# A written-out order of some 1,860 tasks for attention and a gated feed-forward layer on one core: the same tasks in another order, some evictions on another engine, buffers in other slots

## The chip, the cores and the metric

The kernel runs on one core of one Trainium2 chip. The core has engines that each run their own list of instructions in order: TensorE (PE in the profile) multiplies matrices, VectorE (DVE) and ScalarE (ACT) work on the results, GpSimd (POOL) does small elementwise work and issues transfers, SyncE (SP) only issues transfers. Engines meet at semaphores alone: an instruction that waits holds everything behind it on its engine. The metric is the device time of one launch in microseconds (us). Lower is better.

## The reference

Causal attention over 4 batches of 768 tokens with 8 heads of 64 columns, and then a gated layer on the 3072 tokens:

```
mask   = heads 0, 2, 6: all keys up to the query
         other heads:   keys 0 to 3 (sinks), and the last 64 keys
a      = softmax(q k^T / 8, masked)
x      = a v                                    (3072 tokens x 512)
out    = x + sigmoid(x w_res) * ((gelu(x w_gate) * (x w_val)) w_out)
```

with w_gate and w_val of 512 x 1536, w_out of 1536 x 512 and w_res of 512 x 512, all in float32. The kernel computes in float16 with float32 sums.

## The kernel before, in words

**Tiles and stages.** The tokens go in six chunks of 512. A chunk has two halves: *attention* (scores, exp, masks, weighted sums of v, division by the softmax sum, which gives x in token order) and *feed-forward*. Between them x is cast to float16 and turned into feature order (xT), half of it by TensorE transposes (`xT`, L1063) and, in chunks 3, 4 and 5, the other half by a transposing transfer that SP issues (`xD`, L1054). The first chunk's attention is the start of the program; later attention is laid among the feed-forward matmuls of the chunk before it, so that TensorE always has something to do. From the second chunk on, the large products (x with w_gate and w_val, h with w_out) are partly done as seven products of half-size blocks in place of eight, with sums of blocks made on DVE (`wS`, `xS`, `hS`). The gate (`gelu`, `tanh`) is on ACT, the product with the other branch on DVE.

**What is loaded when.** All q, k, v and weight loads are issued by POOL, in its own order (L539). For the first two chunks q and k are turned by TensorE (L682); later ones by transposing transfers on SP (L726). A shifted copy of v, `vs`, is needed where the 64-key window crosses a tile: for the first tiles it is made by DVE or ACT (L617), from the second chunk on by transfers that SP issues (L633). The rows of v for the four sink keys are copied into a small buffer `vk`; for batch 0 these four copies are POOL's (L598), and they need that DVE has cleared that buffer (the memset at L532).

**What sets the order.** `Graph.add` collects tasks, each with an engine, what it depends on and the buffers that it uses. Tasks that could run on two engines (evictions from PSUM, casts, copies) carry alternatives. The string `PLAN` lists every task by number, in one global order; the letter after a number is the engine that is chosen for a task with alternatives (a ACT, d DVE, g POOL, s SP), and `wN` puts N filler matmuls (256 columns of zeros, L1414) on TensorE. `PLACES` gives every buffer its slot in its pool, in the order in which buffers first appear. `schedule` appends each task to its engine's list in the order of `PLAN`; each engine then runs its list in order, and `assign_waits` adds only the semaphore waits that the dependences and the reuse of buffers need.

**Tilings.** A matmul that may run in two halves of 64 columns (`mm`, L477 whole, L478 as a pair) takes the tiling that TensorE is in when its turn comes, so the order also decides where TensorE changes its tiling.

Of the kernel before, what the change touches and what calls it, by code (L numbers as in the profile page):

```python
# [51 lines left out]
    "1 0 14 214 16 210 211 212 215 2 5 w39 240 213 241d w2 228 216 229a w4 230 236 231d 217 237d w6 411 3 6 232 412 4 233d "  # L52
    "200 w4 408 242 409 7 w1 234 243d 238 8 235a 9 239d 10 219 w5 414 410 w1 476 415 11 222 425 416 223 419 224d 426 221 "
    "420 417 422 218 418 225d 427 428 478 421 459 423 477 220 429 424 199 430 w3 442 460 443 413 471 444 431 245 445 432 "
    "472 w1 449 446 447 433 450 255 451 464 462 448 465 434 452 201 453 463 w4 467 461 202 13 435 468 w4 455 436 479 480 "
    "481 466 203 457 456a 437 w1 438 440 458a 482 439d 204 441d w1 473 226d w1 523 474 483 454 205 539 484 538 475 254 227d "
    "522 485 244 503 470 524 505 469 504 540 252 525 207 506 486 541 496 253a 497 488 507 498 206 499 487 514 500 489 501 "
    "266 516 490 17 530 491 267a 256 494 511 531 495d 246 532 492 515 493d 208 502 509 546 508 510a 552 512d 247 533 534 "
    "517 554 209 536 527 556 257 542 558 268 547 548 280 553 550 281 549 526 551 269 555 528 570 529 535 543 537 572 15 576 "
    "594 574 578 544 588 580 545 577 598 559 557 571 590 582 573 584 575 579 586 561 560 564 562 610 592 563 566 581 264 "  # L60
    "568 250 611 265d 296 518 290 589 520 251d 565 287 567 519 289 569 262 198 690 521 295 687 691 12 679 248 591 599 259a "
    "277 680 583 593 585 276 602 688 621 597 293 587 612 622 332 689 670 261a 676 671 674 326 600 249 613 605 623 283 675 "
    "260d 606 624 603 677 625 272 682 595 626 271 681 685 667 601 686 683 284 668 607 672 678 263 614 292 615 684 669 627 "
    "274 632 628 673 616 275 609 617 629 322 692 696 618 697 636 286 633 638 637 634 693 640 639 604 694 641 635 695 698 "
    "714 715 699 642 608 643 258d 700 644d 713 645a 703 701 704 705 649 706 702a 646 707 647 716 718 596 650 648a 709 708 "
    "717 711 710a 652 719 651 722 720 723 653 712d 724 721a 655 725 656 654 740 726 741 727 730 658 731d 728 659 657 729a "
    "747 619 746 660 620 735 770 734 630 742 736 664 631 771 737 273 738 772 752 661 744 754 739 743 662 748 732 745 774 "
    "750 278 663 749 756 775d 785 270 773 776a 777 751 786a 753 787a 755 778 282 796 779 797a 788 781 758 789 799 297 798a "
    "760 800 790 782 792 780 294 757 801 784 793 791 803 783 802 795 285 804 759 794 806 807 762 761 291 808d 805 818 763 "
    "809a 810 829 819d 288 764 811 830a 820d 821 398 831a 812 822 832 813 814 279 328 823 833 824 299 825 306 834 815 298 "  # L70
    "836 835 329 816 826 837 827 848 817 300 828 838 766 320 849 839 765 768 307 767 665 931 397 769 850 343 840 932 852 "
    "844 853 304 851 841 922 856a 924 308 906 845 925 858 847 859 309 843 854 860a 855 842 301 923 864 857d 865 316 846 910 "
    "907 866 926 861 870 911 871 862 914 927 863 928 875 867 929 874 868 909 876 881 310d 908 915 917 912 869 317 882 877 "
    "913 916 342 918 872 934 935 303 936 937 920 878 919 331 942 933 921 938 879 873 939 940 885a 943 323 944 318 880 887 "
    "945 888 946 941a 325 956 952 883 889a 930 957 958 319 884 947 948 953 333 959 949a 954 955 950 960 963 951a 961 965 "
    "315 964 893 886a 966 962a 894 967 330 890 312a 891 313d 895 971 892 969 972a 899 968 666 896 970a 314 897 900 305 976 "
    "1011 981 898 975 327 977 978 979 982 302 980 984 988 311d 1013 983 1012 1015 324 1014 985 987 986 989 990 345 1016d "
    "991 1026 973 992 1018 1027a 993 1017a 995 334 1019 1029 321 904 997 1037 1020 1038a 1021 1022 1028a 994 1030 1039a "
    "1023 903 1040 1024 1031 905 1041 996 1025 1032 998 1042 1048 1033 1000 1044 335 1049a 1034 1045 1035 1043 999 1036 "
    "1046 1051 1001 1047 1050d 1059 1052 1003 1070 1060d 1002 901 1061a 1062 1071a 1054 902 1063 1072a 1005 1004 1064 360 "  # L80
    "1073 1066 1053 1065 1074 336 1007 1055 1075 337 1056 1077 1067 1076 1058 1068 371 1078 1089 1069 1079 347 1009 1057 "
    "1006 1090 358 1008 1080 733 1091 369 1010 384 1166 1081 1093 1167 383 1085 1094 1082 1092 1153 400 1151 1097d 1154 "
    "1159 1095 1086 357 1099 1084 1152 1100 1083 361 1096 1101a 1156 1088 1098a 1163 394 1157 1087 1105 1106 404 1102 1164 "
    "1107 1103 1158 1111 1112 1160 1104 1147 1116 1161 1115 1108 1148 1109 1155 1117 1118 1110 1162 1149 340 1188 1150 1177 "
    "1119 1168 1113 349 1178 1122 1165 1173 1169 1170 1171 350 1179 1172 1189 1184 1185 1120 1174 1180 368 1175 1123 1181 "
    "372 1121 1186 1190 1195 1126d 401 1191 365d 1187 1176d 1124 1125 1192 1114 1183 1182 1197 1128 1127a 1129 1193 1196 "
    "1131 1130a 1198 1132 1194a 370 1199 1134 1135 1133 1203 1136 1201 338 1137 1204d 1202a 1138 1140 1139 1141 1200 1219 "
    "373 1214 1142 1208 1243 1143 1213 359 1145 1220 1245 339 1244 1215 1216 1217 346 1207 1218 1221 354 1222 1246 1223 "
    "1209 355 1210 1224 1211 385 1231 1212 1258 395 1269 1259a 1247 348 1270a 1225 1260a 1248d 1271a 1227 1249d 1250 344 "
    "1272 1251 1261 1233 1273 367 1252 1262 1235 1253 1254 351 1263 1144 1264 1265 1255 1274 1257 1226 366 1276 1266 1206 "  # L90
    "1256 1275 399 1268 1229 1228 1267 1280 1277 341 1281d 1237 1279 1230 1239 974 1282a 1291 1278 352 1283 1238 1292a 1284 "
    "356 1302 1293d 1294 1303a 1285 1295 1240 1241 1205 1287 1305 1304a 1296 1242 1286 353 1306 1288 380 1297 1298 1308 "
    "1289 376 1307 1299 1309 1321 1146 1301 1290 1300 1310 379 1232 1322 1312 1234 388 1311 1402 1323 392 1236 1403 1317 "
    "403 1325 1313 1324 1326 377 363d 1387 1314 1329a 1385 1399 1386 1327 1318 1388 1331 364d 1316 1332 1328 1320 1400 "
    "1333d 1379 1383 1315 1337 1330a 374 1380 1338 1319 1334 381 1401 1335 1384 1339 1393 1390 1381 1343 1336 396 1391 1344 "
    "1382 1404 1340 1348 1405 362a 1389 1406 1394 378 1407 1408 1409 1341 1410 1354 1411 1355 1413 1342 405 1412a 1397 "
    "1358d 1395 1392 1415 1396 1414 1356 1416 1360 1417 1361 1398 1357 1347 1419 1420 1424 1362d 1359a 1349 1425 1418 1421 "
    "1422 1423 1426 1427 1366 1428 1363 1429 375 1367 1364 1430a 1368 1431 1365 1432 1433 1372 1434 1369 1435 1370 1373 "
    "1371 1437 1439 1438a 1350 1440d 1436 1444 1351 1481 1450 1345 1452 1374 1455 1346 1443 1479 513 1445 391 1446 1447 382 "
    "1449 1448 1461 1375 1451 1480 1457 1453 389 1483 1454 1463 1484a 1456 1459 1485d 1486 1465 1458 1487 1679 1494 1442 "  # L100
    "1460 1462 1495a 1482 1488 1464 1490 1489 1496d 1491 1466 1497 1493 1505 390 1498 1467 1492 1499 1506a 1469 1501 386 "
    "1508 1507d 1471 1500 1509 1441 1502 1516 1503 402 1510 1517a 1511 1504 1518a 1468 1512 1519 393 1527 1520 1470 1528a "
    "1513 1529a 1472 1521 1530 387 1515 1522 1523 1514 1473 1531 1524 1538 1525 1533 1539a 1526 1475 406 1532 1540d 1477 "
    "1541 1474 1534 407 1542 1476 1535 1543 1536 1352 1545 1537 1478 1544 1353 1549 1640 1546 1377 1557 1376 1548 1378 1641 "
    "1559 1547 1558 1550 1633 1560 1621 1631 1553 1634 1561 1552 1562 1563 1554 1565a 1564 1556 1632 1567 1551 1568 1566d "
# [1405 lines left out]
```

## Time and profile before

| | |
|---|---|
| time, median of 3 runs | 265.75 us (265.31 to 266.03) |
| profiled execution, span | 264.3 us |
| its time outside the span, by the median | 1.45 us |
| PE busy | 254.5 us (96%) in 3421 matmuls |
| DVE busy | 210.8 us (80%) in 473 instructions |
| ACT busy | 155.3 us (59%) in 274 |
| POOL busy | 106.8 us (40%) in 145 |
| granted TensorE clock, mean | 0.997 of full |

The page divides the span into 40 slices of 6.6 us and gives the busy share of each engine in tenths. An engine's "busy" leaves out the issue of transfers on SP. A row of the waits says which engine stood idle, before which line, and whose end let it go on. The timeline gives the start and the length of groups of instructions in us from the start of the span.

### The profile page before, as it was taken

To read this page: it belongs to the slowest core of one execution; us is meant where nothing else is said; L and a number is where in the kernel's file an instruction comes from. 1 tells how busy PE (TensorE), PEld (TensorE's weight loads), DVE (VectorE), ACT (ScalarE), POOL (GpSimd) and SP (SyncE) were. 2 spreads that over 40 slices of the span, in tenths; PEclk is the share of its full clock that TensorE was granted. 3 is DMA by queue.
4 is the path that set the end of the run, shared out by engine and by line. 5 is a ranking of instruction groups with operands and counts; after the bars stand their busy time and mean duration, and the time that the engine had idled before them with its cause. 6 is when DMAs were issued, how large, how long until landed. Compare 5 with 4: busy or idle time off the path is not lost.

```text
span 264.3 us, 8077 instructions
## 1 busy us (share of the span) xinstructions
PE 254.5 (96%) x3421; PEld 180.7 (68%) x3421; DVE 210.8 (80%) x473; ACT 155.3 (59%) x274; POOL 106.8 (40%) x145
## 2 busy tenths in 40 slices
PE   8999999999999999999998899999999998999993
PEld 5657655558567578667677477579588677778891
DVE  1499555999988978678999677999687976877985
ACT  1277534964554998564883356884655995445511
POOL 8996741990000998013976620711500111110021
PEclk9999999999999999999999999999999999999998
DMA  7999999999297999968999994899589509050004
GB/s 69 166 139 178 207 196 191 188 158 115 82 271 99 141 123 135 182 154 182 136 97 124 152 138 93 200 123 104 69 92 237 101 2 122 7 77 2 2 2 159
DMA packets 102067, 33.17 MB, mean 125 GB/s; under 512 B 88720, under 2 KB 97168, under 8 KB 102032
## 3 DMA queue, kind: packets, MB, share of 16 engines
q0 software_dynamic: 74704, 18.88, 77.3%
q1 hardware_dynamic: 26896, 13.26, 25.0%
q8 instruction: 27, 0.44, 0.7%
q10 hardware_dynamic: 432, 0.52, 0.5%
q14 instruction: 8, 0.07, 0.1%
HBM read 29.36 MB, written 10.49 MB: 151 GB/s over the span
## 4 chain that ended last, share of the span: by engine, by line
PE 87%; DVE 8%; DMA 3%; issue 1%; ACT 0%; DVEq 0%
PE ps L477 45%; PE ps L478 30%; PE ps L850 4%; PE ps L1414 4%; DMA xT<-x 3%; PE ps L682 2%; PE ps L974 2%; PE ps L1063 1%; DVE xtok L1041 1%; DVE x L1039 1%; DVE vk L598 1%; PE ps L941 1%; DVE hS L1251 0%; DVE hT L1228 0%; DVE vs L617 0%
## 5 line engine op out<-in xcount | busy, mean ns | idle before, releaser
L539 POOL DMA_DIRECT2D qks<-in_q_dram x37 | 33.2, 983 | 48.3 <-DMA qT<-qks 26.1
L1359 POOL DMA_DIRECT2D out_dram<-otile x16 | 15.6, 975 | 76.8 <-DVE otile L1355 66.2
L477 PE MATMUL ps<-xT,wg 128*128 128x512 f16 (+1 forms) x172 | 38.7, 337 | 1.4 <-DMA xT<-x 1.0
L477 PE MATMUL ps<-xT,wv 128*128 128x512 f16 (+1 forms) x172 | 38.5, 337 | 0.0
L1129 ACT ACTIVATE gact<-ps 128x512 f16<-128x512 f32 x38 | 22.1, 596 | 27.0 <-PE ps L477 18.0
L1131 DVE SCALAR_TENSOR_TENSOR hT<-gact,ps 128x512 f16<-128x512 f16 x38 | 25.8, 683 | 13.7 <-ACT gact L1129 5.8
L539 POOL DMA_DIRECT2D qks<-in_k_dram x37 | 34.8, 977 | 1.4 <-POOLq L1493 0.8
L1203 DVE TENSOR_TENSOR ps<-ps,otile 128x256 f32<-128x256 f32 x60 | 24.0, 428 | 7.7 <-PE ps L477 3.7
L1221 ACT ACTIVATE gact<-ps 128x512 f16<-128x512 f32 x30 | 16.6, 596 | 15.7 <-PE ps L477 10.8
L539 POOL DMA_DIRECT2D va<-in_v_dram x24 | 23.7, 1017 | 3.8 <-DVE va L534 3.8
L477 PEld LDWEIGHTS ps<-xT,wg 128*128 128x128 f16 x172 | 16.2, 98 | 13.1 <-DMA xT<-x 1.5
L477 PEld LDWEIGHTS ps<-xT,wv 128*128 128x128 f16 x172 | 16.6, 98 | 11.4 <-issue 0.2
L866 ACT ACTIVATE ea<-ps 128x1024 f16<-128x1024 f32 (+2 forms) x24 | 22.0, 925 | 1.4 <-PE ps L850 1.3
L1228 DVE SCALAR_TENSOR_TENSOR hT<-gact,ps 128x512 f16<-128x512 f16 x30 | 19.3, 682 | 2.6 <-PE ps L478 1.2
L1299 ACT ACTIVATE srs<-ps 128x512 f32<-128x512 f32 x22 | 13.1, 599 | 12.2 <-PE ps L478 7.8
L477 PE MATMUL ps<-wo,hT 128*128 128x256 f16 (+1 forms) x114 | 18.3, 296 | 0.0
L478 PE MATMUL ps<-xT,wg 128*64 128x512 f16 (+1 forms) x144 | 17.6, 344 | 0.0
L478 PE MATMUL ps<-xT,wv 128*64 128x512 f16 (+1 forms) x144 | 17.6, 344 | 0.0
L1041 DVE TENSOR_TENSOR xtok<-ps,rcp 128x512 f32<-128x512 f32 (+1 forms) x28 | 16.8, 608 | 0.6
L1331 DVE TENSOR_TENSOR otile<-otile,ps 128x256 f32<-128x256 f32 x33 | 13.1, 412 | 3.7 <-PE ps L477 2.4
L850 PE MATMUL ps<-qT,kT 64*128 64x64 f16 (+4 forms) x391 | 15.9, 213 | 0.1
L478 PE MATMUL ps<-wo,hT 128*64 128x256 f16 x216 | 15.6, 273 | 0.4 <-DVE otile L1325 0.4
(175 smaller groups left out, 590.4 us busy)
## 6 DMA issues: line engine op xcount, KB each, us to landing
out_dram<-xtok SPq DMA_DIRECT2D x4, 1024.0 KB, 4.8
out_dram<-otile POOLq DMA_DIRECT2D x16, 256.0 KB, 4.5
va<-in_v_dram POOLq DMA_DIRECT2D x24, 128.0 KB, 5.6
qks<-in_k_dram POOLq DMA_DIRECT2D x32, 64.0 KB, 4.9
qks<-in_q_dram POOLq DMA_DIRECT2D x32, 64.0 KB, 5.0
wv<-in_moe_w_val_dram POOLq DMA_DIRECT2D x3, 512.0 KB, 13.2
wg<-in_moe_w_gate_dram POOLq DMA_DIRECT2D x3, 512.0 KB, 11.4
wo<-in_moe_w_out_dram POOLq DMA_DIRECT2D x4, 384.0 KB, 20.9
```

What stands on the lines that cost most here:

```text
L477: return e.matmul(o, lhsT=lhsT, rhs=rhs, **k)
L478: return [e.matmul(o[h:h + 64], lhsT=lhsT[:, h:h + 64], rhs=rhs, **k) for h in (0, 64)][-1]
L539: return G.add(eng, issue, lambda e: e.dma_start(out_ap(), in_ap), deps, prio, bufs=bufs, dma=cost, name=name, grp=grp)
L850: return [e.matmul(at(scr)[:, oo:oo + w], lhsT=side(BB, qb, low, 1)[half, k0:k0 + 128], rhs=side(BB, qb, low, 0)[half, qq:qq + w], start=T ...
L866: return e.activation(out=o, in_=i_, func=AF.Exp, scale=SM_SCALE)
L1041: t2 = G.add("dve", c_dve(2 * n * 64), lambda e: e.tensor_tensor(out=xview(), in0=avv(0, DHEAD), in1=scale(), op=ALU.mult), [t1] + xdeps, ...
L1129: ta = G.add("act", c_act(512), (lambda gb=gb, ga=ga, gw=gw: lambda e: e.activation(out=at(ga)[:, :], in_=at(gb)[:, gw], func=AF.Gelu))(), ...
L1131: th = G.add("dve", c_dve(512), (lambda vb=vb, ga=ga, f=f, vw=vw: lambda e: e.scalar_tensor_tensor(out=hv(f), in0=at(ga)[:, :], scalar=0.5 ...
L1203: return G.add("dve", c_dve(256), lambda e: e.tensor_tensor(out=at(ps)[:, o], in0=at(ps)[:, BL], in1=at(es)[:, 0:256], op=ALU.add), deps, ...
L1221: ta = G.add("act", c_act(512), (lambda x=x, ga=ga, both=both: lambda e: e.activation(out=two(at(ga)[:, :]), in_=both(x), func=AF.Gelu))() ...
L1228: th = G.add("dve", c_dve(512), (lambda x=x, f=f, ga=ga, both=both: lambda e: e.scalar_tensor_tensor(out=two(hv(f)), in0=two(at(ga)[:, :]) ...
L1359: t = G.add("pool", 1.0, (lambda ot=ot, r0=r0: lambda e: e.dma_start(out[r0:r0 + 128, :], at(ot)[:, :], accum_op=ALU.add))(), ends + [stor ...
```

## The change

Two tables of numbers are replaced, `PLAN` and `PLACES`. No task is added to the work or taken from it, except fillers: 55 in place of 77. The first lines of the two tables, which stand for all of them:

```diff
 PLAN = (
-    "1 0 14 214 16 210 211 212 215 2 5 w39 240 213 241d w2 228 216 229a w4 230 236 231d 217 237d w6 411 3 6 232 412 4 233d "
+    "0 210 16 211 213 212 1 2 w20 228 230 w3 234 214 17 231 229a 411 235 408 412 5 232 233 w12 419 215 409 240 6 3 7 217 4 "
...
 PLACES = (
-    "0 2 0 0 0 1 0 0 1 1 1 2 3 0 0 2 0 3 0 1 1 1 1 3 1 0 0 0 1 0 1 1 1 0 0 0 2 0 2 1 1 0 1 1 1 0 1 0 0 2 0 2 0 1 0 0 1 1 0 "
```

In numbers: fillers 77 to 55 (39 to 20 before the first real matmul); changes of TensorE's tiling 104 to 94, all ten of them before the first w_gate product; 22 matmuls whole before and now pairs; DVE 475 to 461 instructions and ACT 279 to 290, mostly copies that move from DVE to ACT; the last additions of the residual on POOL are in four pieces of 256 columns and one of 512, where there were two and one. The table being one line shorter, every line number of the changed kernel is smaller by one (L539 becomes L538).

**First place: POOL at the start**, which issues all loads. `qks` receives q and k, `va` is v, `wg`, `wv`, `wr`, `wo` are the four weights. Before, from the first weights on:

```order
L539 DMA wv<-in_moe_w_val_dram 128x4x512
L497 AFFINE_SELECT m_win<-m_win 128x256
L497 AFFINE_SELECT m_win<-m_win 128x64
L525 MEMSET m_win 128x64
L497 AFFINE_SELECT m_win<-m_win 128x64
L539 DMA va<-in_v_dram 128x8x64
L598 COPY vk<-va 4x130 x3
L539 DMA va<-in_v_dram 128x8x64
L598 COPY vk<-va 4x130
L539 DMA wg<-in_moe_w_gate_dram 128x4x512
L539 DMA qks<-in_q_dram 128x8x128 x2
L539 DMA wg<-in_moe_w_gate_dram 128x4x512
```

and now:

```order
L538 DMA va<-in_v_dram 128x8x64 x2
L538 DMA qks<-in_q_dram 128x8x128
L538 DMA wg<-in_moe_w_gate_dram 128x4x512
L597 COPY vk<-va 4x130 x4
L538 DMA qks<-in_k_dram 128x8x128
L538 DMA wv<-in_moe_w_val_dram 128x4x512
L538 DMA wg<-in_moe_w_gate_dram 128x4x512
L538 DMA qks<-in_q_dram 128x8x128
L538 DMA wv<-in_moe_w_val_dram 128x4x512
L538 DMA wg<-in_moe_w_gate_dram 128x4x512
```

All four copies into `vk` now stand in one place, behind the first part of w_gate and ahead of every other weight; the first part of w_val has moved behind them. The memset of DVE on which they wait is the third instruction of DVE's list before, and the 23rd now; ahead of it there now are seven evictions of q and k, masks, and copies of v.

**Second place: TensorE between the attention of chunk 3 and the first product that reads its transfer-transposed half** (`vk,ek` are the last sums that this half of x waits for, `xT,wg` and `xT,wv` the first products). Before, the last such sum stands 32 rows above the product that waits for the transfer; the last rows of this stretch are:

```order
L477 MATMUL ps<-vk,ek 128x65 x3
L477 MATMUL ps<-wo,hS 128x256 x4
L477 MATMUL ps<-wo,wS 128x256 x2
L477 MATMUL ps<-wo,hT 128x256 x6
L1063 MATMUL ps<-ident,x 128x128 x8
L477 MATMUL ps<-wo,hT 128x256 x6
L477 MATMUL ps<-wt,hT 128x256 x6
L477 MATMUL ps<-xT,wg 128x512 x2
L477 MATMUL ps<-xT,wv 128x512 x4
L477 MATMUL ps<-xT,wg 128x512 x2
L477 MATMUL ps<-xT,wv 128x512 x2
L477 MATMUL ps<-xT,wg 128x512 x2
```

and now the whole stretch, from those sums to the product that waits (the second half of the last row):

```order
L476 MATMUL ps<-vk,ek 128x65 x9
L1062 MATMUL ps<-ident,x 128x128 x8
L476 MATMUL ps<-wt,hS 128x256 x4
L476 MATMUL ps<-wt,wS 128x256 x2
L476 MATMUL ps<-wt,hS 128x256
L476 MATMUL ps<-wt,wS 128x256 x2
L476 MATMUL ps<-xT,wg 128x512 x4
L476 MATMUL ps<-wo,hT 128x256 x6
L476 MATMUL ps<-wo,hS 128x256 x4
L476 MATMUL ps<-wo,wS 128x256 x2
L476 MATMUL ps<-xT,wv 128x512 x2
L476 MATMUL ps<-wt,hT 128x256 x6
L476 MATMUL ps<-xT,wv 128x512 x4
```

The sums have moved down to just above the transposes, so that fewer matmuls lie between the end of the attention and the product. In chunk 4 the stretch shrinks likewise, from 72 to 42 half-width matmuls of 256 columns and from 84 small sums to none, with 16 of 512 columns in both; in chunk 5 from 72 and 92 to 42 and none, with 16 and 24 of 512 columns.

**Third place: SP around that transfer** (`xT<-x`). Before:

```order
L1054 DMA_TRANSPOSE xT<-x 128x8x128
L726 DMA_TRANSPOSE kT<-qks 128x4x128 x2
L726 DMA_TRANSPOSE qT<-qks 128x4x128 x2
L726 DMA_TRANSPOSE kT<-qks 128x4x128
L633 DMA vs<-va 64x2x455
```

and now:

```order
L736 DMA q<-qT 64x256
L1280 DMA out_dram<-xtok 128x4x512
L1053 DMA_TRANSPOSE xT<-x 128x8x128
L632 DMA vs<-va 64x455
L725 DMA_TRANSPOSE qT<-qks 128x4x128
L632 DMA vs<-va 64x2x455
```

The transfer is still issued once per chunk; its neighbours on SP have changed. In chunk 3 the cast of x that it needs, last of what it waits for before, has moved from DVE (L1048) to ACT (L1046).

150 rows, old and new, of tables (PLACES, PLAN) are left out of this document.

## The prediction

> **What bounds the kernel now.** I read the page first (busy shares, slices, chain), then the waits of PE, then the timeline around the longest of them.
>
> ```profile
> span 264.3 us, 8077 instructions
> PE 254.5 (96%) x3421; PEld 180.7 (68%) x3421; DVE 210.8 (80%) x473; ACT 155.3 (59%) x274; POOL 106.8 (40%) x145
> PE   8999999999999999999998899999999998999993
> PE 87%; DVE 8%; DMA 3%; issue 1%; ACT 0%; DVEq 0%
> ```
>
> PE is busy in every slice but the first and the last, and it is 87% of the chain that ended last. So time is PE's work plus what PE waits. The waits of PE (engine, tile, line; who ended the wait; us in total, times, longest):
>
> ```profile
> PE ps L1414 <- DVE blank L511: 1.2, 1, 1.2
> PE ps L478 <- issue: 1.1, 1, 1.1
> PE ps L477 <- DMA xT<-x: 1.0, 1, 1.0
> PE ps L1063 <- DVE x L1039: 0.7, 1, 0.7
> PE ps L478 <- DVE otile L1325: 0.4, 1, 0.4
> PE ps L477 <- DVE xtok L1041: 0.4, 1, 0.4
> PE ps L478 <- DVE hS L1251: 0.3, 1, 0.3
> PE ps L478 <- DVE otile L1331: 0.2, 1, 0.2
> ```
>
> They are few and short, 5.3 us together, and that is all that an order can remove; what it can add has no such ceiling. Beside them the start costs time, since PE's dense work begins only with the first w_gate and w_val products. PE's timeline, and PE's work in stretches (start:end, its length, busy us and matmuls of PE):
>
> ```profile
> 1.21 7.03 PE L1414 MATMUL ps<-blank 128*128 128x256 f16 x39 [1.21 <-DVE blank L511]
> 22.26 1.03 PE L477 MATMUL ps<-xT,wv 128*128 128x256 f16 x8
> 23.67 1.03 PE L477 MATMUL ps<-xT,wg 128*128 128x256 f16 x8 [0.38 <-DVE xtok L1041]
> ...
> 1.20:6.50 5.30, 5.29 (x25) 3.78 (x26) 1.00 0.90 84
> 6.50:8.16 1.66, 1.66 (x16) 1.30 (x13) 1.00 1.70 162
> ```
>
> Thirty-nine fillers hold PE until 8.16, where the first transposes start; the first 25 take 0.21 us each (5.29/25), the later ones 0.104 (1.66/16). From this second row I price the rest: 256 columns 0.104 us, 512 twice that, 128 half; a pair of half-width matmuls counts as one.
>
> **The change part by part.** The real matmuls are the same; so the sum starts from 264.3 and asks, place by place, which waits go and which come.
>
> *The start.* Fillers go from 77 to 55, and 20 stand first instead of 39. The cover for this is DVE, not PE:
>
> ```profile
> 2.44 0.81 POOL L539 DMA_DIRECT2D qks<-in_k_dram  x1
> 8.62 0.69 DVE L693 COPY kT<-ps 128x512 f16<-128x512 f16 x1 [6.58 <-PE ps L682]
> 14.28 0.41 DVE L902 TENSOR_TENSOR ea<-ea,m_causal 128x512 f16<-128x512 f16 x1
> 23.10 0.42 DVE L1041 TENSOR_TENSOR xtok<-ps,rcp 128x256 f32<-128x256 f32 x1
> ```
>
> (The first row is POOL's first load.) DVE starts with the first eviction at 8.62, works without a gap from 14.28, and its xtok releases the first w_gate product. Now PE reaches its first transposes some 2.3 us earlier, since 20 fillers at 0.21 end at 5.4 and the loads of q and k, whose issue starts at 2.44 either way, are the next limit. But DVE's list up to the x that this product needs is only 3 instructions shorter (34 for 37, by 0.4 us each 1.2 us at most), and behind it come a transpose and an ACT eviction. If all of the earlier start arrived, the first w_gate product would start at 23.67 - 2.3 = 21.4; if none, at 23.67. I take 23.0, nearer to the late end, since DVE has no gap in which to catch up. The work ahead of it is the same on both sides: 8 w_val products less (8 x 0.104 = 0.8 us), 16 transposes and 16 short sums more (0.8 us). Term: **-0.7**, bounds -2.3 and +0.5. It contains the 0.4 on xtok. Ten changes of tiling fewer lie in this same stretch, under DVE's cover, and count nothing.
>
> *POOL's copies into vk.* These now wait for DVE's 23rd instruction, and all weights but the first part of w_gate are queued behind them. The trace has such a stop of POOL, later:
>
> ```profile
> 12.51 0.94 POOL L598 COPY vk<-va 4x130 f16<-4x130 f16 x3
> 17.27 0.77 POOL L539 DMA_DIRECT2D wg<-in_moe_w_gate_dram  x1
> 28.09 1.78 POOL L539 DMA_DIRECT2D va<-in_v_dram  x2 [3.84 <-DVE va L534]
> ...
> wv<-in_moe_w_val_dram POOLq DMA_DIRECT2D x3, 512.0 KB, 13.2
> wg<-in_moe_w_gate_dram POOLq DMA_DIRECT2D x3, 512.0 KB, 11.4
> wo<-in_moe_w_out_dram POOLq DMA_DIRECT2D x4, 384.0 KB, 20.9
> ```
>
> DVE's work ahead of that memset is seven evictions at 0.69 (4.8), masks and copies of v (some 4.6) and gaps as before (1.6): from about 6.3 it ends near 17.5. Four copies at 0.31 (0.94/3) bring POOL to 18.8, where the second part of w_gate was issued at 17.27 before; with a k load ahead of w_val and about 0.8 us for each issue, the first part of w_val goes out near 20.5 (9.43 before) and w_gate's second near 21.3, four us later. The long times to landing (11 to 21 us) are queueing, and the queue runs empty in the stop, so much of the four us comes back. Stretched over the products in their new order this leaves each weight some 1 to 3 us ahead of its first use. Bounds 0 and +1.5 (one weight late by half its lead twice); I take **+0.2**.
>
> *The second chunk's vs copies* wait for v loads that stand behind those weights. The transfers of SP at L633 take this long to landing (min/median/max of 14):
>
> ```profile
> L633 SPq DMA_DIRECT2D vs<-va x14: 485/609/650, 46.6 to 204.3; - x14
> DMA to landing us min/median/max: 2.0/4.3/7.3
> ```
>
> Their v loads land near 55 to 56 by the same shift, so the copies at 58 to 63 by this row, and the first windowed sums come on PE at about 61. Wait: bounds 0 and 2.5, median landing 0; I take **+0.9**.
>
> *The transposed half of x.* These rows (start, length of the issue; then to landing of the three) carry the largest term:
>
> ```profile
> 142.46 1.24 SPq L1054 DMA_TRANSPOSE xT<-x  x1
> 180.85 1.23 SPq L1054 DMA_TRANSPOSE xT<-x  x1
> 221.41 1.52 SPq L1054 DMA_TRANSPOSE xT<-x  x1
> DMA to landing us min/median/max: 3.7/4.9/7.4
> 179.85 0.20 DVE L1028 RECIPROCAL rcp<-ps 128x8 f32<-128x8 f32 x1
> 180.08 0.69 DVE L1039 TENSOR_TENSOR x<-ps,rcp 128x512 f16<-128x512 f32 x1
> 149.86 0.61 PE L477 MATMUL ps<-xT,wg 128*128 128x512 f16 x2 [1.05 <-DMA xT<-x]
> ```
>
> The first took 7.4 us and PE waited 1.05 for it at 149.86; the third took 3.7. Before, 7 us and more of matmuls covered each. Now, in chunk 3, from the last sum to the waiting product lie 8 of 128 columns (0.4), 27 of 256 (2.8) and 8 of 512 (1.7): 4.9 us. Of that some 1.2 us pass before the issue (DVE's reciprocal and scaling take from 179.85 to 180.77 ahead of the issue at 180.85, and 0.2 to 0.3 go from the sum's end to their start), so 3.7 are cover. At 3.7 to landing PE waits 0, at 7.4 it waits 3.7; loads of the next chunk are still in flight there as before, but fewer right ahead of it: half, **+1.85** in place of the 1.0 that goes. In chunk 4, 21 pairs of 256 and 8 of 512 are 3.85, less 1.2 is 2.7: at 3.7 it waits 1.0, at 4.9 2.2; SP has no transpose just ahead, as at 221.41, so **+1.0**. In chunk 5 the same counting gives 5.1 - 1.2 = 3.9 of cover: 0, up to +1.0.
>
> *Other waits.* The 0.7 on x (L1039) and the 0.3 and 0.2 on hS and otile (L1331) lie where the order is wholly different, and I take them as gone: **-1.2** (0 if they come again elsewhere). ACT makes more of the copies that refill PSUM for a following sum; the shortest such loops are about 0.2 us shorter in matmuls than before: **+0.3**, up to 1. The issue stall of 1.1 and the end stay: the last products and their tail are in the same order.
>
> *Sum.* 264.3 - 0.7 - 1.0 - 1.2 + 0.2 + 0.9 + 1.85 + 1.0 + 0.3 = 265.65 us of span. The profiled execution's span stands 1.45 below the median of the runs (265.75), so the time is 267.1 us.
>
> [...] The rows show that the granted clock column reads 1.00 while the first 25 fillers run at half the later rate, up to 6.5 us. [...]
>
> **The rivals.** *One: the transfers land in time (faster).* At 3.7 us the transposed half costs 0 and 1.0, the vs copies and the weights are ahead: 265.65 - 1.85 - 0.9 - 0.2 = 262.7, and with 0.3 less in ACT's loops 262.4; time 263.9. For it: the third transfer's 3.7, and fewer transposes on SP behind the one of chunk 3. Against: 7.4 under load, and chunk 3 still has load.
>
> *Two: POOL's stop decides (much slower).* If DVE's memset comes 3 us later than worked out, or the queue does not catch up, w_val and w_out come late one after the other: from a delay beyond 3 us on, each us counts once. Two us there, 2.5 on vs and 3.7 in chunk 3: 265.65 + 1.8 + 1.6 + 1.85 = 270.9, time 272.3. For it: landing times up to 20.9 behind a full queue.
>
> *Three: the array is cold longer.* A start in which real matmuls run at 0.21 instead of 0.104 per 256 columns adds about half of 5.5 us of early PE work; DVE covers most, so the first w_gate product comes at 24.5 instead of 23.0: 267.15, time 268.6. Against it: PE has 35 more fillers to bridge gaps.
>
> *Four: no change.* What goes and what comes cancel, with 0.5 in chunk 3 where I took 1.85: 264.3, time 265.7.
>
> **How the numbers follow.** Forecast 0.36, rival one 0.34, rival two 0.10, three 0.04, four 0.16. A measurement tells 0.3% (0.8 us) from no change. Faster is rival one (0.34), same is rival four (0.16), slower the rest (0.50). The range goes from 262.2, below rival one for a start at 21.9 in place of 23.0, to 271.4, where chunk 3 waits its 3.7, vs 2.5 and chunk 4 2.2 (265.65 + 1.85 + 1.6 + 1.2 = 270.3, plus 1.45, less the 0.35 by which not all come at once). The forecast's own range is 266.5 to 269.
>
> **What would show each step.** In the changed profile: the first w_gate row near 23.0 with a wait on ACT or DVE of at most 0.5; POOL idle before `vk` for 2 us or more, released by DVE vk; waits of PE on DMA xT<-x of 1 to 3 us in two places, and one on vs near 61; none on wg, wv, wr, wo above 0.5. If PE waits for x less than 0.5 us in all, rival one is right. If waits on weights exceed 2 us, rival two. The prediction as a whole is wrong if the time lies below 265, or if a wait of over 2 us stands at a place that is not named here.

## The result, and the profile after

The changed kernel takes **276.56 us** (median of 4 runs, 275.79 to 277.46) against 265.53 us before on the same chip: a ratio of **1.040**, 95% interval 1.036 to 1.045. It is 11 us slower. The forecast was 267.1 us in a range of 262.2 to 271.4: the sign was right, the size was not, and the range does not hold the time.

The page of the profile after (span and busy time; then PE and the clock granted to it in 40 slices, here of 6.9 us; then the chain by engine):

```profile
span 275.4 us, 8061 instructions
PE 255.9 (93%) x3419; PEld 181.6 (66%) x3419; DVE 203.8 (74%) x459; ACT 160.3 (58%) x286; POOL 107.8 (39%) x147
PE   7789999976999999999999399999999997999992
PEclk9999999995999999999999779999999999999999
PE 66%; DMA 14%; POOL 9%; DVE 6%; issue 2%; SPq 1%; ACT 0%; POOLq 0%; DVEq 0%
```

Transfers, 3% of the chain before, are 14% now. PE has two holes, one near 60 and one near 152 us, and at the same places the clock row falls to 5 and to 7, where before it was full but for the last slice. The waits of PE name the holes:

```profile
PE ps L476 <- DMA xT<-x: 4.5, 1, 4.5
PE ps L973 <- DMA vs<-va: 4.1, 1, 4.1
PE ps L1062 <- issue: 1.6, 1, 1.6
PE ps L1413 <- DVE blank L510: 1.1, 1, 1.1
PE ps L681 <- DMA qks<-in_q_dram: 1.1, 2, 0.9
PE ps L477 <- DVE otile L1330: 0.7, 1, 0.7
```

Both are places that the prediction had: the vs copies of the second chunk, and the transfer-transposed half of x in chunk 3. What it did not have stands in PE's work by stretches (start:end, length; PE busy and matmuls; the number ahead of the last two, which are the transfers' share and rate, is the granted clock):

```profile
62.00:64.37 2.37, 0.00 (x0) 0.00 (x0) 0.00 (x0) 0.00 (x0) 0.00 (x0) 0.59 1.59 145
64.37:66.00 1.63, 1.63 (x48) 1.56 (x49) 0.00 (x0) 0.00 (x0) 0.00 (x0) 0.50 0.55 92
66.00:68.00 2.00, 2.00 (x19) 1.57 (x17) 1.53 (x4) 0.28 (x1) 1.82 (x3) 0.50 0.11 13
68.00:70.00 2.00, 2.00 (x19) 1.60 (x18) 0.67 (x2) 0.94 (x3) 2.00 (x3) 0.69 1.53 98
...
156.20:158.00 1.80, 1.78 (x6) 0.87 (x7) 0.76 (x2) 0.00 (x0) 0.00 (x0) 0.50 1.86 188
158.00:160.00 2.00, 2.00 (x7) 0.88 (x6) 0.51 (x1) 0.60 (x1) 0.00 (x0) 0.50 1.20 312
160.00:162.00 2.00, 2.00 (x7) 0.78 (x6) 1.98 (x6) 0.60 (x1) 0.00 (x0) 0.65 0.96 302
```

Behind each hole TensorE runs at half its clock for about 5 us (0.50 until 69.24 and until 161.40). By the clock's share, in the first 1.63 x 0.5 + 2.0 x 0.5 + 2.0 x 0.31 = 2.4 us of work is not done; in the second 0.9 + 1.0 + 0.7 = 2.6. So the two places cost 4.1 + 2.4 and 4.5 + 2.6, together 13.6 us, 12.6 more than before (which waited 1.0 for x). The start gives back 1.2 (the first w_gate product at 22.51 in place of 23.67, below). Small waits of 1.6 are gone (0.7 on x, 0.4 on otile, 0.5 on hS and otile), and 1.2 came new (0.7 on otile, 0.5 more of the issue stall). 12.6 - 1.2 - 1.6 + 1.2 = 11.0, and the span grew by 11.1.

The start went nearly as predicted. The first row is PE's first w_gate product, the second POOL's copies into vk (start, length, idle time before and who ended it):

```profile
22.51 1.04 PE L476 MATMUL ps<-xT,wg 128*128 128x256 f16 x8
17.23 1.30 POOL L597 COPY vk<-va 4x130 f16<-4x130 f16 x4 [3.33 <-DVE vk L531]
```

### The profile page after: what moved, and what is told of

It is laid out like the page before. It is cut to its first block, busy times and chain, and to the rows that moved or that the text cites. A ratio compares the mean times of both kernels' runs of the same rounds, so it can differ in the third digit from the quotient of the medians.

```text
span 275.4 us, 8061 instructions
## 1 busy us (share of the span) xinstructions
PE 255.9 (93%) x3419; PEld 181.6 (66%) x3419; DVE 203.8 (74%) x459; ACT 160.3 (58%) x286; POOL 107.8 (39%) x147
## 4 chain that ended last, share of the span: by engine, by line
PE 66%; DMA 14%; POOL 9%; DVE 6%; issue 2%; SPq 1%; ACT 0%; POOLq 0%; DVEq 0%
PE ps L476 33%; PE ps L477 27%; DMA va<-in_v_dram 8%; DMA xT<-x 4%; PE ps L849 3%; POOL qks L538 3%; DMA vs<-va 2%; PE ps L973 1%; POOL va L538 1%; DVE otile L1354 1%; PE ps L1062 1%; POOL wo L538 1%; SPq L632 1%; POOL wv L538 1%; DVE xtok L1040 1%
## 5 line engine op out<-in xcount | busy, mean ns | idle before, releaser
L538 POOL DMA_DIRECT2D qks<-in_q_dram x37 | 32.4, 1026 | 29.7 <-DMA kT<-qks 13.9
L476 PE MATMUL ps<-xT,wg 128*128 128x512 f16 (+1 forms) x172 | 39.6, 343 | 0.0
L538 POOL DMA_DIRECT2D qks<-in_k_dram x37 | 34.0, 1018 | 5.8 <-issue 4.9
L538 POOL DMA_DIRECT2D va<-in_v_dram x24 | 25.9, 1087 | 13.1 <-PE ps L973 13.1
L476 PEld LDWEIGHTS ps<-xT,wv 128*128 128x128 f16 x164 | 15.8, 99 | 15.9 <-DMA xT<-x 5.0
L477 PE MATMUL ps<-xT,wv 128*64 128x512 f16 (+1 forms) x160 | 20.5, 342 | 0.0
L476 PE MATMUL ps<-wo,hT 128*128 128x256 f16 (+1 forms) x114 | 19.2, 303 | 0.0
L477 PE MATMUL ps<-xT,wg 128*64 128x512 f16 (+1 forms) x144 | 18.7, 344 | 0.1
L1198 ACT ACTIVATE ps<-ps 128x256 f32<-128x256 f32 x26 | 9.7, 371 | 14.8 <-PE ps L476 9.4
L1325 ACT ACTIVATE otile<-ps 128x256 f32<-128x256 f32 x22 | 8.4, 388 | 16.5 <-PE ps L476 8.8
L849 PE MATMUL ps<-qT,kT 64*128 64x64 f16 (+3 forms) x391 | 16.3, 213 | 0.5 <-DVE qT L692 0.5
```

Source lines behind the costliest of these rows:

```text
L476: return e.matmul(o, lhsT=lhsT, rhs=rhs, **k)
L477: return [e.matmul(o[h:h + 64], lhsT=lhsT[:, h:h + 64], rhs=rhs, **k) for h in (0, 64)][-1]
L538: return G.add(eng, issue, lambda e: e.dma_start(out_ap(), in_ap), deps, prio, bufs=bufs, dma=cost, name=name, grp=grp)
L849: return [e.matmul(at(scr)[:, oo:oo + w], lhsT=side(BB, qb, low, 1)[half, k0:k0 + 128], rhs=side(BB, qb, low, 0)[half, qq:qq + w], start=T ...
```

## The experiments

The theories. **A**: the two long waits themselves bring TensorE to half clock; **B**: the half clock has another cause. **P**: POOL's stop at vk makes vs late; **Q**: the transfers' own traffic does. **C**: the transfers are slow because others share the transfer engines with them; **D/E**: they are slow by themselves. **R**: the order brings PE to a place too early. **S**: the two places are the whole loss; **T**: the order is tight everywhere, and what one place gives back the next takes. All edits are to the order (or add a dependence); some lengthen the file, so line numbers differ by up to 6. Each ratio is to the kernel before on the same chip; the change itself has 1.040 (1.036 to 1.045).

### Fillers in the holes: the half clock

A token `u3.36` puts 36 fillers at that place, into a PSUM bank that is free there.

```diff
-    ... 641 329 325 713 722 ...
+    ... 641 329 325 u3.36 713 722 ...        (713: first windowed sum that waits for vs)
-    ... 1125 1204a 1207 1181 ...
+    ... 1125 1204a u3.38 1207 1181 ...       (ten products ahead of the one that waits for x)
```

First edit alone:

> The changed kernel with 36 more filler matmuls (256 columns, 0.109 us each, 3.9 us) on TensorE right ahead of the first windowed sum of the second chunk, which waits 4.1 us for vs. Nothing else moves. Theory A (an idle stretch of 4 us itself brings TensorE to half clock, which then costs some 2.3 us until 69.4): the wait becomes fillers and the sum still starts near 64.4, but the clock reads 1.00 from there to 70; the time falls by 2.0 to 2.5 us, from 276.6 to about 274.3, though work was added. Theory B (the half clock there has another cause than idleness, such as the time since the start): the clock still reads 0.50 from 64 to 69 and the time is unchanged, within 0.3.

Second alone:

> The changed kernel with 38 more fillers (4.1 us) on TensorE some 3.5 us ahead of the first product of chunk 3 that waits for the transfer-transposed half of x (4.5 us at 151.7). Nothing else moves. Theory A (idleness brings the half clock): the wait shrinks to about 0.4, the product still starts near 156.2, the clock stays 1.00 behind it, and the time falls by 2.3 to 2.8 us, to about 274. Theory B: no change, or slower by up to 0.5 where the pushed products hold DVE up.

Both:

> Both sets of fillers, 74 in all. Theory A: the two gains add, 4.4 to 5.2 us, to about 271.8; what remains against the kernel before (some 6 us) is the bare waits. If the gains do not add, the second half clock does not come from its own idle stretch. Theory B: 276.6 or slower.

Measured: 272.94 us, ratio 1.029 (1.023 to 1.036) for vs; 273.82 us, 1.035 (1.029 to 1.041) for x; 273.09 us, 1.031 (1.027 to 1.035) for both. With both, and by a hair with the first alone, the kernel gets faster by *adding* matmuls; the run for x alone is not told apart from the change by its time. The same stretches of the first run, ahead of the sums and behind them, and then the waits on transfers of the run with both:

```profile
60.00:65.00 5.00, 4.22 (x39) 3.54 (x37) 1.26 (x3) 1.18 (x3) 0.00 (x0) 1.00 1.68 145
65.00:67.00 2.00, 1.61 (x56) 1.52 (x57) 0.31 (x3) 0.00 (x0) 0.29 (x1) 1.00 0.48 93
67.00:70.00 3.00, 3.00 (x38) 2.75 (x37) 3.00 (x7) 1.94 (x5) 3.00 (x4) 1.00 0.79 51
```

```profile
PE ps L483 <- DMA xT<-x: 1.1, 1, 1.1
PE ps L979 <- DMA vs<-va: 0.4, 1, 0.4
```

vs still comes as late (65.3 for 64.3), yet the clock reads 1.00 in all three rows where it read 0.50 to 0.69. **A holds, B falls**: at these two places the idleness makes the half clock. What it cost can be timed on the same matmuls: from the first of these sums to the last eight transposes of the stage they take 7.21 us in the changed kernel and 5.00 here, 2.2 us; at x, from the product that waited to the first `wS,wgt`, 6.0 in place of 3.5 (second run), 2.5 us. The two figures worked out above, 2.4 and 2.6, were near; with the timed ones the account there comes to 10.7 of the 11.1 us.

The gains do not add. In the first run's profiled execution x lands earlier and its wait is 3.3 us, with the clock at 1.00 behind it, so there the 38 fillers have no half clock to save; that execution has the highest mean clock of its four (0.999; the others 0.981 to 0.993). With both in, the granted clock is 0.996 to 1.00 in all four executions, and most of what is left, 3.1% or 8 us, is the length of the two holes, now filled: 8.6 us, where the kernel before waited 1.0.

### POOL's stop

```diff
-    "0 210 16 211 213 212 1 2 w20 ...  226 14 w7 ..."
+    "0 210 16 211 213 212 1 2 14 w20 ...  226 w7 ..."
```

> The changed kernel with DVE's memset of vk, the 23rd instruction of its list, moved to the 4th, so that POOL's four copies need not wait (3.3 us of POOL's stop go). Theory P (POOL's stop is what makes vs late): all loads behind come 3.3 us earlier, vs with them; the 4.1 us wait falls to about 0.8, below what brings the half clock, and the time falls by 5 to 6 us to about 271. Theory Q (the transfers behind one another are the limit, and the queue, which ran empty only from 20.1 to 21.3, takes most of it back): the loads land 1.2 us earlier, the wait falls to about 2.9, and the time falls by 1.2 us, or 3.5 if the half clock goes with it.

Measured: 274.95 us, 1.038 (1.031 to 1.046), not told apart from the change. POOL's row of this run:

```profile
16.16 1.53 POOL L597 COPY vk<-va 4x130 f16<-4x130 f16 x4 [2.23 <-DMA va<-in_v_dram]
```

With the memset out of the way the copies wait for their v load instead, and only 0.9 us is won; vs lands no earlier (65.7), and PE waits 4.7. So the run did not test P. The next one took the stop out for good, with the copies behind six loads:

```diff
-    ... 223 426 468 ...                                  (223, 220 to 222: the copies)
+    ... 254 200 201 245 202 203 223 426 468 ...          (and 14 early, as above)
```

> The changed kernel with POOL's stop taken out altogether: DVE's memset of vk early, and the four copies into vk behind the next six loads (k, the first and second part of w_val, two of w_gate, q), so that POOL never stands still ahead of a weight. In the last run the memset alone did not do it: the copies then waited for their v load until 16.2, and vs came no earlier. Theory P (the stop makes vs late): the second k load goes out at 14 instead of 18.5, vs lands 3 us earlier or more, the 4 us wait goes, time down by 5 us or more to about 271. Theory Q (the transfers are limited by what moves, not by when POOL issues): the loads land 1 to 1.5 us earlier, vs lands near 63, the wait stays near 3 and the time falls by 1 to 1.5 us, or by 3.5 where the half clock goes as well.

Measured: 274.81 us, 1.033 (1.021 to 1.044). The first k load behind the stop goes out at 13.88 in place of 18.49, 4.6 us earlier, and the last vs copy lands at 62.98 in place of 64.33: 1.35 us. **Q, as to the transfers.** Of the 4.6 us that POOL gains the copies see 1.35, as Q had it; that the queue behind the stop is the limit fits this and is not shown further. The time, not told apart from the change, does not show Q's gain: PE no longer waits for vs, not because vs is early but because PE is late (at the sums at 63.08, where it stood waiting from 60.27). Stretches from the start of this run:

```profile
12.00:14.00 2.00, 1.69 (x26) 1.06 (x26) 1.97 (x4) 0.81 (x3) 2.00 (x4) 0.57 1.90 115
14.00:16.00 2.00, 2.00 (x18) 1.16 (x17) 1.70 (x5) 1.03 (x2) 2.00 (x3) 0.58 1.65 123
22.00:24.00 2.00, 1.78 (x33) 1.55 (x29) 1.96 (x8) 1.35 (x5) 2.00 (x4) 0.63 1.27 214
24.00:26.00 2.00, 2.00 (x32) 1.64 (x27) 1.28 (x5) 1.49 (x2) 2.00 (x3) 0.52 1.28 196
```

The clock fell back twice in the start, where PE has only short gaps, the longest 1.1 us. That is the third rival of the prediction, in this execution; two of the runs below (x alone, and everything behind x held) show it too, from 21.3 to 24.7 us.

### The sums later in PE's order

```diff
-    ... 329 325 713 722 635 703 717 702a 644a 705 704 718 642 608 719 643 724 646 647 ...
+    ... 329 325 642 643 644a 646 647 713 722 635 703 717 702a 705 704 718 608 719 724 ...
```

> The changed kernel with four groups of output products of the first chunk (12 matmuls of 256 columns, 1.3 us) ahead of the windowed sums that wait for vs instead of behind them, as in the kernel before, where two of these groups stood ahead. Theory R (the order brings TensorE to these sums too early; the transfer is as it is): the wait falls by 1.3 us from 4.1 to 2.8 and the half clock behind it goes: 64.4 to 70 at clock 1.00, and the time falls by 2.3 us, since the bare wait only changes places with work, plus the 1.3. If the half clock stays at 2.8 us of idleness, the fall is 1.3.

Measured: 274.38 us, 1.035 (1.027 to 1.042). The wait on vs is 3.1 us, and the clock stays at 1.00 behind it; at x, a wait of 3.8 brings it to half. Both rows of this run, just behind the two waits:

```profile
66.00:68.00 2.00, 1.49 (x37) 1.12 (x31) 1.31 (x4) 0.34 (x1) 1.30 (x2) 1.00 0.05 9
156.00:158.00 2.00, 2.00 (x8) 0.91 (x6) 0.87 (x2) 0.68 (x2) 0.00 (x0) 0.50 1.46 237
```

**R holds for the place** (the order brings PE there too early), and this hole of 3.1 us did not cost its second part. The whole gain of 2.3 did not arrive: by the ratios it is 1.6 (0.006 x 266), within the intervals.

### What makes the transfers slow

One dependence each: for x, POOL's first of nine loads waits for the scaling that the transposing transfer waits for too; for vs, the first of eleven small loads waits for PE's first sum of that stage.

```diff
+        for a_, b_ in ((395, 1181),):            (x)     or  ((289, 692),):       (vs)
+            self.tasks[a_].deps.append(self.tasks[b_])
```

> The changed kernel with nine loads of q, k and v of POOL (issued from 144.2 to 150.1) made to wait for the scaling of x that the transposing transfer of chunk 3 also waits for: they go out behind that transfer instead of ahead of it. Theory C (the loads in flight make the transfer slow, 7.8 us to landing instead of 3.0): it lands in 3.5 to 5 us, the wait of 4.5 at 151.7 falls to 1 to 2, the half clock behind it goes, and the time falls by 5 to 6 us to about 271. Theory D (the transfer is slow by its own neighbours on SP or its kind): it takes 7 us still and the time is unchanged.

> The changed kernel with eleven small loads of q and k (issued from 46.4 to 52.2, ahead of the four vs transfers) made to wait for the first sum of TensorE in that stage (57.4). Theory C (contention): the vs transfers take 4 to 5 us to landing instead of 6.5 to 7, the last lands near 62, the wait falls to about 1.8 without a half clock, and the time falls by 4 to 4.5 us. Theory E (vs is late because its v loads land only at 54.9 and SP issues one transfer after the other): the last still lands near 64 and the time is unchanged, or worse by what the loads now are late.

Measured: x alone 273.77 us, 1.032 (1.024 to 1.039); vs alone 272.19 us, 1.029 (1.021 to 1.037). The transposing transfer's longest time to landing (min/median/max of the three; the first row is the changed kernel's, the second this run's), and then the row of PE's longest waits with vs alone:

```profile
DMA to landing us min/median/max: 3.0/3.1/7.8
```

```profile
DMA to landing us min/median/max: 3.0/3.5/5.6
```

```profile
PE ps L478 <- DMA xT<-x: 3.7, 1, 3.7
PE ps L478 <- DVE ps L1204: 3.6, 3, 2.7
PE ps L1064 <- issue: 1.6, 1, 1.6
```

**C holds at vs**: issued at the same time (54.92 to 58.3), the four copies land at 58.8, 59.3, 59.5 and 60.2 in place of 61.7 to 64.3, 2.5 to 3.9 us each instead of 6.6 to 7.6, and no wait for vs is left. At x the same step takes the transfer from 7.8 to 5.6; that shows little, since in the seven other runs of this order in which no load was held at x it took 5.5 (with the fillers at x) to 7.3. But with vs 6.5 us should have come back and by the ratios 3 did. The row on DVE shows one place where the rest went: near 125 a DVE copy waits 2.9 us for an output transfer to leave its buffer (the new places: this buffer's next user comes soon), PE waits 2.7 for the copy, and the clock is at 0.50 from 126 to 128 again.

### Both at once, and more fillers

```diff
+        for a_, b_ in ((395, 1181), (289, 692)):
-    ... 1031 905 1009 ...
+    ... 315 351 905 368 ...                       (905: that output transfer; 368: a load that stops POOL)
```

> The changed kernel with both sets of loads held back, the eleven ahead of vs and the nine ahead of the transposing transfer, and with one output transfer of POOL (the one whose buffer a DVE copy takes again near 125) ahead of a load that stops POOL until 115. Account to be tested: of the 11 us, the wait on vs with its half clock is 6.4, the wait on x with its half clock 7.2 less the 1.2 that the kernel before had there; each goes in full or but for 2 us. Theory S (these two places are the whole of it): about 276.6 - 6.4 - 4.8 = 265.4, within 1% of the kernel before, with waits of PE on vs of 0, on x below 2.5, and the clock at 1.00 from 30 us on. Theory T (the order is tight all along, and what one place gives back the next takes): above 269, with new waits of 1 to 3 us on DVE or on buffers.

and, with `w3` to `w10` and `w2` to `w6` at the start:

> The run before this one, with eleven more fillers in the first 14 us (10 and 6 where 3 and 2 stand), where PE has gaps of 0.4 to 0.9 us. In two runs above, the clock read 0.5 to 0.8 between 12 and 26 us although no gap there was longer than 0.9. Theory F (with 55 fillers in place of 77 the start is too thin, and the clock falls back in some executions): the clock stays 1.00 at the start in all executions, the first w_gate product comes no later, and the median falls by 0.5 to 1.5 us with less scatter. Theory G (the fillers do nothing for it): the same median or up to 0.5 slower.

Measured: 273.32 us, 1.025 (1.019 to 1.031), and 271.46 us, 1.020 (1.017 to 1.023). **T rather than S**: 3.9 us of waiting on x are still there, and small waits have come up all along, on DVE, on a weight and on a moved piece of kT (`q<-kT`):

```profile
PE ps L478 <- DMA xT<-x: 3.9, 1, 3.9
PE ps L478 <- DVE ps L1204: 2.1, 3, 1.0
...
PE ps L851 <- DMA q<-kT: 1.4, 1, 1.4
...
PE ps L478 <- DMA wv<-in_moe_w_val_dram: 1.0, 1, 1.0
```

These rows are of the first of the two. Its transfer took 7.2 us although the nine loads went out behind it (0.3 us behind), so the holding of the loads had been timed too finely to decide C at x. Whether the fillers at the start helped stays open: the intervals overlap.

### Everything behind the transfer

What is issued behind the transposing transfer, POOL's nine loads and SP's own next transfers, waits until it has landed; alone, and with all of the above:

```diff
+        for a_, b_ in ((395, 1183), (367, 1183)):          (and (289, 692), 905 and the fillers as above)
```

> The changed kernel with everything that is issued behind the transposing transfer of chunk 3, POOL's nine loads and SP's next transfers, made to wait until it has landed. Holding back the loads alone gave 5.6 us to landing in one run and 7.2 in the next, in place of 7.8. Theory C (whatever shares the transfer engines with it makes it slow, also what is issued after it): it lands in 3 to 4 us, the wait on x is below 1 with no half clock behind it, and the time falls by 5 to 7 us in place of 3. Theory D (its own queue or what was issued ahead makes it slow): 5.5 us or more as before, and the time is not below that of the run with loads held.

> That, with the eleven loads ahead of vs held back, the output transfer moved up on POOL and the eleven more fillers at the start: all that was found. Theory S (vs, x and the half clocks behind them are the loss): 276.6 - 6.4 - 6.0 - 0.7 = 263.5, within 1% of the kernel before. Theory T (the order leaves so little slack that other waits take the place): 268 or more, with at least 4 us of waits of PE on DVE, on qT and kT transfers and on weights.

Measured: 279.78 us, 1.052 (1.044 to 1.059), and 278.82 us, 1.050 (1.042 to 1.059): the slowest of all. Yet the transfer itself is what C said. Its times to landing, alone and then with all, and PE's two longest waits with all:

```profile
DMA to landing us min/median/max: 3.1/3.1/4.9
```

```profile
DMA to landing us min/median/max: 3.0/3.0/4.6
```

```profile
PE ps L851 <- DMA kT<-qks: 6.9, 1, 6.9
PE ps L478 <- DMA xT<-x: 1.3, 1, 1.3
```

**C holds at x**: 4.9 and 4.6 us are below the 5.5 to 7.8 of every run of this order in which nothing was held there, and the wait is 1.6 and 1.3 with the clock at 1.00 behind it. Why it is not the 3.0 of chunks 4 and 5 stays open. The transfers that were held back are the next chunk's k and q, and PE then waits 6.2 and 6.9 us for kT, until 177.6 and 174.0, longer than it ever waited for x, with half clock for 6.8 us from 174.9 and 172.1. This new hole comes from the hold itself, so these two runs do not decide between S and T; they show that what is held back for x has to land soon as well. A shorter hold was not run.

### Two runs of the kernel before

One part of the change alone, 20 fillers for 39:

```diff
-    "1 0 14 214 16 210 211 212 215 2 5 w39 240 ...
+    "1 0 14 214 16 210 211 212 215 2 5 w20 240 ...
```

> The kernel before with 20 fillers at the start in place of 39, all else as it was: one part of the change alone. By the prediction (DVE covers the start) the first w_gate product comes at 21.4 to 23.7 and the time changes by -1 to +0.3 us. By the third rival (the array is cold longer) the clock reads below 1.00 between 8 and 26 us, the first w_gate product comes 0.5 to 1.5 us later, and the time rises by as much.

Measured: 266.64 us, 1.001 (0.997 to 1.004). No change, with the first w_gate product 1.6 us earlier and the clock at 1.00 from 8 to 26 us in the profiled execution, so the third rival does not show here. Its row in the timeline, and from the waits the longest on a transfer behind it:

```profile
22.07 1.05 PE L477 MATMUL ps<-xT,wg 128*128 128x256 f16 x8 [0.17 <-DVE x L1039]
```

```profile
PE ps L941 <- DMA qT<-qks: 1.5, 1, 1.5
```

What PE wins at the start it waits later, in this execution: 0.6 us for a moved piece of kT at 92.7, 0.6 for x at 185.8 and 1.5 for qT at 206.8, less the 1.0 for x at 149.9, which is gone: 1.7 in all.

And the step that the runs on x point to: in the kernel before, the transposing transfer of chunk 3 was held until 142.46 by a cast that stood behind two copies on DVE. The cast goes ahead of them:

```diff
-    ... 1195 1126d 401 1191 365d 1187 1176d 1124 ...      (1176: the cast; 1126, 365: the copies)
+    ... 1195 1176d 1126d 401 1191 365d 1187 1124 ...
```

> The kernel before, with the cast of x for chunk 3 on DVE ahead of two copies that stood before it (0.4 and 0.8 us): the transposing transfer, which waited for this cast until 142.46, can go 1.1 us earlier. If the transfer's start decides (the wait of 1.0 at 149.86 is behind it), it lands 1.1 earlier, the wait goes, and the time falls by 0.8 to 1.1 us, to 0.996 to 0.997 of the kernel before. If the traffic decides when it lands, it takes longer by as much and the time is unchanged.

Measured: **264.25 us, 0.9935 (0.9905 to 0.9965)**: faster than both kernels. The transfer goes out at 140.98 and lands at 146.38 (142.46 and 149.82 before), and no wait for x is left among PE's:

```profile
PE ps L1414 <- DVE blank L511: 1.2, 1, 1.2
PE ps L478 <- issue: 1.1, 1, 1.1
PE ps L478 <- DVE otile L1325: 0.4, 1, 0.4
PE ps L477 <- DVE xtok L1041: 0.2, 1, 0.2
```

It gained 1.7 us by the ratio (0.9 to 2.5) where 0.8 to 1.1 was expected: beside the wait of 1.0 for xT, that of 0.7 for x on DVE just ahead of it, at 144.7, is gone. The transfer also took 5.4 us instead of 7.4, but that need not come from the edit: in the run with fewer fillers it went out at 142.34, as before, and took 5.4 as well.

## Why the prediction was right or wrong

*What bounds the kernel* was right: PE's work plus PE's waits, and the loss is where PE waits. *"What it can add has no such ceiling"* was right as well and was then not used: the range was cut at 271.4. (Its other end does not come out of its reason: a start at 21.9 for 23.0 takes 1.1 from rival one's 263.9, which is 262.8 and not 262.2.)

*The start*: predicted -0.7 with the first product at 23.0; it came at 22.51. DVE's memset was forecast near 17.5 with the copies done at 18.8; they ran from 17.23 and POOL went on at 18.49. The weights were in time (0.2 forecast; no wait of PE on a weight is among its rows, only 0.4 on the copies into vk and 0.2 on a v load, both ahead of that product). But the run with fewer fillers in the kernel before shows that such an earlier start need not be worth its 1.6 us: waits on later transfers took it back.

*The vs copies*: forecast +0.9, upper bound 2.5; measured 4.1. Two errors. The sum let the copies land up to 63, but the row quoted for it said 7.3 at most, and the last two of the four were issued at 57.1 and 57.7; they took 6.6 to 7.0. And the place in the kernel before had been just in time (the last copy landed 0.3 us ahead of its use), which the step did not look up: every us by which PE comes sooner and the copies later is then a us of waiting.

*The transposed half of x*: forecast +1.85 for chunk 3, upper bound 3.7; measured 4.5. The cover was 3.3, not 3.7 (the last sum ends at 146.61 and the issue follows 1.8 later, not 1.2), and the transfer took 7.8. "Half" of the two ends was taken because fewer loads stood right ahead of it; but loads and SP's transfers *behind* it slow it too: with all of them held it took 4.9 and 4.6. In chunk 4 it was too dark: 1.0 forecast, 3.0 us to landing and a wait of 0.1. In chunk 5 none, as said.

*The step that failed most is none of these terms but one that is missing*: each wait was priced at its own length. The two long ones cost 2.4 and 2.6 us more, since the clock fell to 0.50 behind them; the runs with fillers show it. Of the 9.5 us by which the forecast fell short these are 5.0, the vs copies 3.2 and chunk 3 2.65, less 1.4 where chunk 4 and the start came out better than forecast. The trace before shows such a fall as well, at its end, where the last matmul ends at 260.15 and the clock is at half from 262.55 on; no step of the prediction used it:

```profile
262.55:264.30 1.75, 0.00 (x0) 0.00 (x0) 0.00 (x0) 0.00 (x0) 0.00 (x0) 0.50 0.36 138
```

The 5.3 us until the later rate, from the prediction's rows (1.20 to 6.50), are those of one execution: in the changed kernel's the first 16 fillers take 0.20 us each (3.24/16, from 1.14 to 4.38) and those from 4.38 on 0.10 (0.81/8).

*The rivals.* The second (POOL's stop decides, 272.3) was nearest in time and wrong in mechanism: the stop can be taken out and only 1.35 us of landing follow. The first and the fourth fell. The third (cold start) is not what made the change slow, but it happens: with the copies behind the loads the clock read 0.5 to 0.6 twice in the start, and in two other runs once. That fewer fillers bring it about was the author's estimate; the run of the kernel before with 20 of them does not show it. The places were named ahead, "waits of PE on DMA xT<-x of 1 to 3 us in two places, and one on vs near 61"; it was one place, of 4.5, and vs at 60 to 64. By its two signs of being wrong as a whole (a time below 265, a wait of over 2 us at a place not named) the prediction would have stood: they ask for the place of a wait and not for its size.

## What to carry to other kernels

The two long waits of TensorE had two prices here: their length (4.1 and 4.5 us), and the half clock behind them (2.2 and 2.5 us, as timed). So in an order that is already dense, look for the one hole of 4 us before four of 1 us that lie apart (behind the start, no hole below 2.5 us cost the clock here), and try matmuls on nothing in a long idle slot that cannot be avoided (at vs they brought the ratio from 1.040 to 1.029). Before bringing a consumer of a transfer forward, look up by how much its last transfer was ahead of it, and price the transfer at the longest time its row shows, with what is issued behind it counted as well as what is ahead (7.8 us to landing here, 4.9 with what is behind it held). Where later transfers are only just in time, an earlier start or a transfer put first may only move the wait to one of them.

## What the runs showed of the hardware that was not expected

The length of a hole alone does not tell whether it costs the clock. In the profiled executions the clock fell to half behind waits of 3.7 (vs alone, at x), 3.8 (sums later, at x), 3.9 (fillers at x, at vs), 4.1, 4.5 and above; it stayed at 1.00 behind 3.1 (sums later, at vs), 3.3 (fillers at vs, at x), 3.8 (memset early, at x) and 3.9 (both sets of loads held, at x); and it fell behind 2.5 (x alone, at vs) and 2.7 (vs alone, near 125).

What decides was not shown. In the changed kernel the half clock lasted 6.83 us at both places (62.41 to 69.24 and 154.57 to 161.40). PE's busy time in stretches of half that length, two rows each of the changed kernel and of x alone, both at vs, and then three of the run with both sets of loads held, at x:

```profile
59.00:62.41 3.41, 1.27 (x14) 0.62 (x12) 2.21 (x5) 1.39 (x3) 0.00 (x0) 1.00 1.95 183
62.41:65.82 3.41, 1.45 (x44) 1.38 (x45) 0.00 (x0) 0.00 (x0) 0.00 (x0) 0.50 1.12 120
62.21:65.63 3.42, 1.34 (x54) 1.28 (x55) 0.56 (x3) 0.44 (x2) 0.03 (x1) 1.00 1.23 129
65.63:69.04 3.41, 3.41 (x23) 2.52 (x21) 2.25 (x6) 1.29 (x3) 3.41 (x5) 0.50 0.78 53
149.31:152.72 3.41, 1.48 (x10) 0.78 (x8) 1.45 (x3) 0.00 (x0) 3.41 (x6) 1.00 1.42 99
152.72:156.13 3.41, 1.39 (x9) 0.88 (x10) 0.76 (x2) 0.00 (x0) 1.99 (x3) 1.00 2.05 166
156.13:159.54 3.41, 3.41 (x22) 1.90 (x21) 2.76 (x7) 2.01 (x5) 0.00 (x0) 1.00 1.40 289
```

The clock fell behind rows in which PE was busy for 37% (the hole of 4.1 us) and 39% (that of 2.5 us); it stayed at 1.00 behind the two rows over which the hole of 3.9 us is split, with 43% and 41%. These are three places, so that the share decides is the author's estimate, and no limit is shown. The start does not follow it: with x alone PE was busy 1.40 and 1.74 of 2.00 us from 18 to 22, and the clock fell at 21.3, while from 10 to 14 it was busy 1.41 and 1.38 and the clock stayed at 1.00; why is open.

A transfer's time to landing about doubled with company here. The transposing transfer took 3.0 to 3.1 us in chunks 4 and 5 of most runs of the changed order (in the changed kernel with a transfer share of 0.46 around it in chunk 4) and 5.5 to 7.8 in chunk 3 (there 1.6 to 1.9), and 4.6 to 4.9 in chunk 3 once what is issued after it was held back. The four vs copies took 2.2 to 3.9 us in the four runs in which the loads ahead of them were held back, and 5.7 to 8.5 in all others.
